# Attention products on 64-row groups, two PSUM banks per tile, units of four and five tokens, and routing in two halves

## The chip, the cores and the metric

The kernel runs on one core of one Trainium2 chip. The metric is the device time in microseconds of one execution. TensorE is called PE below, VectorE DVE, ScalarE ACT, GpSimd POOL and the DMA-issuing SyncE SP.

## The reference

Eight batches of eight heads with 576 positions of 64 elements, all in float32:

```python
def sm_attn(qq, kk, vv):
    s = scale * np.matmul(qq, kk.transpose(0, 1, 3, 2))
    s = s - np.max(s, axis=-1, keepdims=True)
    a = np.exp(s)
    a = a / (np.sum(a, axis=-1, keepdims=True) + 1e-09)
    return np.matmul(a, vv)
p_packed = sm_attn(p, k, v)              # 32 pooled keys for each head
out = sm_attn(q, p_packed, p_packed)     # 576 x 32 scores for each head
# x = out as (4608, 512); each token goes to its best expert of 8
expert_idx = np.argmax(xn @ en.T / tau, axis=1)
out[mask] = gate_w[mask, None] * (np.maximum(x[mask] @ w1[e], 0.0) @ w2[e])
# then a dense gated layer: (x @ w_a) * (x @ w_b) @ w_out
```

## The kernel before

The kernel has three stages. **Attention** (function `attention`) takes the batches one after another and leaves, for each, the normalized weights `a` of the second softmax (to `a_dram`) and the transposed pooled keys `ppT` (to `pT_dram`). The attention output itself is never formed: since out = a times p_packed, the first expert product is a times (p_packed times w1). **Experts** (class `Moe`, functions `zed`, `up_mm`, `down_mm`) runs 16 slots of 288 tokens, two per batch; `zed` makes z = p_packed times w1 once for each batch. It assumes that all tokens of a batch go to one expert, whose number SP reads into a register, and a slower path (`Dense`) is taken if that fails. **The gated layer** (class `Moe2`) follows; the change leaves it alone.

The order on each engine is fixed when the program is built: `Sched.run` places operations one after another, by planned durations, priorities (`prio`) and the number of free buffers (`take` and `free`). Each engine then works its list in order, and so does SP's queue of DMA issues.

In the attention stage `prep(b)` transposes pooled queries (`pT_mm`, L252) and keys (`kT_mm`, L272), forms the first scores (`s1_mm`, L302 and L307), takes their exponentials, transposes these (`eT_mm`, L356), multiplies by the values (`pp_mm`, L373), and makes `ppT` (L398) and the small Gram matrix `gr` (L412, L413, L417). `query(b)` transposes the queries (L458) and calls `rest(b, w)` for units of three tokens (a token here is one position index i of 9 on 64 partitions, for two halves of the partitions): second scores `s2_mm` (L496), maximum (L502), subtraction (L506), exponential (L510), sum and reciprocal (L514, L515), normalization (L519), transposition (L525), and the product `x_mm` (L539) with `gr`, from which squared norms (L548, L553) and router dots are taken. `experts(b)` (L672, L691 to L721) then routes one batch.

In the products for scores, for `x` and for `z`, one operand holds 64 useful rows per head. `s1_mm`, `s2_mm` and `zed` use all 128 rows of the array with zeros in the other half: `pz`, `pT` and `ppT` are padded with zeros so that a head of the lower or the upper half is picked by which half is zero. `x_mm` uses 128 rows with a block-diagonal `gr` of four blocks. Only `pp_mm` and `gr_mm` use 64-row groups. In the trace a 32-bit matmul other than a transposition makes two records, each with its own weight load.

PSUM has eight banks. In the attention stage four single banks are `tr` (transpositions, first scores, `gr`, routing, the first batch's z), two are `sm` (second scores, and the two halves of `pp`), two are `x`. In the experts stage three pairs of banks are `up`, two single banks are `dn`.

Of the kernel before, what the change touches and what calls it, by code (L numbers as in the profile page):

```python
# [22 lines left out]
NI = NT // 64  # L23
AHEAD = 0.65
QA = 1.5
# [9 lines left out]
def make_consts(nc, c, keep, pool, emb, tau, psum, en, esq):  # L35
# [7 lines left out]
    c.blk = pool.tile([128, 4, NP], F32, name="blk")  # L43
    nc.gpsimd.memset(c.blk, 0.0)
    for j in range(4):
        nc.gpsimd.memset(c.blk[32 * j:32 * j + 32, j, :], 1.0)
# [103 lines left out]
NW = CI // 3  # L150


def attention(ctx, tc, c, q, k, v, p, a_dram, pT_dram, consts, more):
    nc = tc.nc
    W = 4 * NP + E
    sizes = dict(tr=4, sm=2, x=2, k=3, v=3, q=3, qT=4, e=2, eT=2, a=2, an=3, aT=2, sq=2, pz=2, pT=2, kt=1,
                 pc=2, gr0=2, gr1=2, ppT0=2, ppT1=2, **{f"kT{m}": 1 for m in range(4)})
    sb = {}
    for name, pools in dict(io="kvq", kt=["pT", "kt"] + [f"kT{m}" for m in range(4)], q=["qT"], e=["e", "eT"],
                            pp=["pc", "gr0", "gr1", "ppT0", "ppT1"], x=["a", "an", "aT", "sq"]).items():  # L160
# [4 lines left out]
    ps_pool = dict(tr=c.ps_tr, sm=c.ps_sm, x=c.ps_x)  # L165
    pzs = [sb["pT"].tile([128, 2, 3 * D], F32, name=f"pz{i}") for i in range(2)]
    for t in pzs:
        nc.vector.memset(t, 0.0)
# [7 lines left out]
    own["a"] = [sb["a"].tile([128, 12, NP + 1], F32, name=f"as{i}") for i in range(sizes["a"])]  # L176
    for g in range(2):
        own[f"ppT{g}"] = [sb["pc"].tile([128, 4, 2, NP], F32, name=f"ppT{g}{i}") for i in range(sizes[f"ppT{g}"])]
        for t in own[f"ppT{g}"]:
            nc.gpsimd.memset(t, 0.0)  # L180
# [16 lines left out]
    def psum(n, key):  # L197
        T_[key] = ps_pool[n].tile([128, 512], F32, tag=n, name=n)
# [22 lines left out]
    def prep(b):  # L221
# [5 lines left out]
        def load_p(e):  # L227
            turn_ = T_["pz", b] = pzs[b % 2]
            nc.sync.dma_start(out=turn_[:, :, D:2 * D], in_=p[b].rearrange("(g j) p d -> (j p) g d", j=4))
# [17 lines left out]
        def pT_mm(e):  # L247
            ps = psum("tr", ("pTp", b))
            tile_("pT", ("pT", b), [128, 2, 2, 128])
            for g in range(2):  # L250
                for a in range(2):
                    nc.tensor.transpose(  # L252
                        ps[:, (2 * g + a) * 128:(2 * g + a + 1) * 128], T_["pz", b][:, g, (1 - a) * D:(3 - a) * D],
                        c.ident)

        def pT_ev(e):
            copy(e, T_["pT", b], T_["pTp", b].rearrange("p (g a q) -> p g a q", g=2, a=2))

        t, bpT = Buf("tr"), Buf("pT")
        o = op({"T": 0.44}, pT_mm, deps=[o_p], prio=at(0), take=[t, bpT], free=[bp])  # L260
        o_pT = op({"A": 0.47, "V": 0.6}, pT_ev, deps=[o], prio=at(0), free=[t])
# [28 lines left out]
        for g in range(2):  # L290
            def s1_mm(a, g=g):
                def f(e):
                    ps = psum("tr", ("s1p", b, g, a))
                    if (g, a) == (0, 0):
                        tile_("e", ("e", b), [128, CI, 2, D])

                    def w(j):
                        h = 2 * j + g
                        return T_["pT", b][:, h // 4, a, h % 4 * 32:h % 4 * 32 + 32]

                    for j in range(4):
# [3 lines left out]
                    if a == 0:  # L305
                        for j in range(4):
                            nc.tensor.matmul(  # L307
                                ps[32 * j:32 * j + 32, 256:320], lhsT=w(j),
                                rhs=T_["kT", b, 4][:, j, 64 * g:64 * g + 64], start=True, stop=True)
# [1556 lines left out]
```

## Time and profile before

| | us |
|---|---|
| median of 3 runs | 1373.44 (1370.06 to 1374.18) |
| the profiled execution | 1371.34 |
| its span, first to last instruction | 1369.5 |
| busy in the span: PE | 1335.0 |
| DVE | 790.8 |
| ACT | 591.9 |
| POOL | 106.5 |

The busy time of PE counts a matmul from its start to its modelled end, so that pipelined matmuls overlap in it; how long a matmul occupies PE is read from the start of one group to the start of the next. The clock column of the stretches is the granted share of full speed.

### The profile page before, as it was taken

To read this page: it belongs to the slowest core of one execution; us is meant where nothing else is said; L and a number is where in the kernel's file an instruction comes from. 1 tells how busy PE (TensorE), PEld (TensorE's weight loads), DVE (VectorE), ACT (ScalarE), POOL (GpSimd) and SP (SyncE) were. 2 spreads that over 40 slices of the span, in tenths; PEclk is the share of its full clock that TensorE was granted. 3 is DMA by queue.
4 is the path that set the end of the run, shared out by engine and by line. 5 is a ranking of instruction groups with operands and counts; after the bars stand their busy time and mean duration, and the time that the engine had idled before them with its cause. 6 is when DMAs were issued, how large, how long until landed. Compare 5 with 4: busy or idle time off the path is not lost. (4 is left out here: it accounts for less than half of the span.)

```text
span 1369.5 us, 26692 instructions
## 1 busy us (share of the span) xinstructions
PE 1335.0 (97%) x10263; PEld 1214.9 (89%) x10263; DVE 790.8 (58%) x1635; ACT 591.9 (43%) x1222; POOL 106.5 (8%) x234
## 2 busy tenths in 40 slices
PE   8998989999999999999999999999999999999997
PEld 6767778999999998999899999999999989999996
DVE  5787867666766655798554356434634363444342
ACT  5656524444444434565533244234433442343232
POOL 1121210101001000000100010001000010001001
PEclk9999999999999999999999999999999999999999
DMA  8878366778876735777865576557655665556552
GB/s 286 279 244 258 119 223 228 253 241 262 289 247 200 238 116 187 254 254 268 254 170 162 162 232 176 161 157 221 188 160 160 206 199 159 160 166 198 160 161 65
DMA packets 169272, 278.04 MB, mean 203 GB/s; under 512 B 16937, under 2 KB 68521, under 8 KB 169137
## 3 DMA queue, kind: packets, MB, share of 16 engines
q1 hardware_dynamic: 162704, 257.35, 60.9%
q0 software_dynamic: 6272, 18.88, 4.0%
q8 instruction: 84, 1.38, 0.4%
q14 instruction: 52, 0.42, 0.1%
q10 hardware_dynamic: 160, 0.02, 0.0%
HBM read 219.04 MB, written 57.15 MB: 202 GB/s over the span
## 5 line engine op out<-in xcount | busy, mean ns | idle before, releaser
L1443 DVE TENSOR_TENSOR s<-s,s 128x384 f32<-128x384 f32 x324 | 176.8, 556 | 340.8 <-ACT s L1579 338.4
L765 PE MATMUL pb<-xq,wq 128*128 128x384 f32 x504 | 170.2, 338 | 1.5 <-DVE s L1443 0.7
L765 PE MATMUL pa<-xq,wq 128*128 128x384 f32 x504 | 169.6, 337 | 1.6 <-DVE s L1443 1.6
L1692 PE MATMUL o<-oh,gh 128*128 128x512 f32 x432 | 170.3, 394 | 0.9 <-ACT osb L1712 0.9
L1693 PE MATMUL o<-ol,gh 128*128 128x512 f32 x432 | 170.4, 394 | 0.0
L1694 PE MATMUL o<-oh,gl 128*128 128x512 f32 x432 | 170.4, 394 | 0.0
L767 PE MATMUL pa<-xq,wq 128*128 128x384 f32 x504 | 170.3, 338 | 0.0
L767 PE MATMUL pb<-xq,wq 128*128 128x384 f32 x504 | 170.1, 337 | 0.0
L766 PE MATMUL pb<-xq,wq 128*128 128x384 f32 x504 | 170.0, 337 | 0.0
L766 PE MATMUL pa<-xq,wq 128*128 128x384 f32 x504 | 169.9, 337 | 0.0
L765 PE MATMUL dn<-hh,w2h 128*128 128x288 f32 x512 | 153.0, 299 | 0.0
L1579 ACT COPY s<-pa 128x384 f32<-128x384 f32 x180 | 86.5, 481 | 149.9 <-PE pa L767 149.8
L767 PE MATMUL dn<-hh,w2l 128*128 128x288 f32 x512 | 151.0, 295 | 0.0
L766 PE MATMUL dn<-hl,w2h 128*128 128x288 f32 x512 | 150.3, 294 | 0.0
L1579 ACT COPY s<-pb 128x384 f32<-128x384 f32 x180 | 86.5, 481 | 140.7 <-PE pb L767 140.6
L765 PEld LDWEIGHTS dn<-hh,w2h 128*128 128x128 f32 x512 | 96.1, 188 | 11.7 <-ACT w2h L994 5.9
L765 PEld LDWEIGHTS pb<-xq,wq 128*128 128x128 f32 x504 | 94.7, 188 | 11.8 <-DVE c L1443 1.6
L765 PEld LDWEIGHTS pa<-xq,wq 128*128 128x128 f32 x504 | 94.7, 188 | 10.0 <-DVE s L1443 2.2
L766 PEld LDWEIGHTS pb<-xq,wq 128*128 128x128 f32 x504 | 94.6, 188 | 8.4
L766 PEld LDWEIGHTS pa<-xq,wq 128*128 128x128 f32 x504 | 94.6, 188 | 7.5
L1694 PEld LDWEIGHTS o<-oh,gl 128*128 128x128 f32 x432 | 81.0, 187 | 18.8
L766 PEld LDWEIGHTS dn<-hl,w2h 128*128 128x128 f32 x512 | 96.8, 189 | 0.0
(192 smaller groups left out, 2436.1 us busy)
## 6 DMA issues: line engine op xcount, KB each, us to landing
wq<-ws SPq DMA_DIRECT2D x420, 256.0 KB, 2.8
ws<-wq SPq DMA_DIRECT2D x84, 256.0 KB, 3.7
raw<-in_moe_w_dram SPq DMA_DIRECT2D x36, 512.0 KB, 6.2
rawb<-in_moe_w_dram SPq DMA_DIRECT2D x28, 512.0 KB, 9.1
k<-in_k_dram SPq DMA_DIRECT2D x16, 576.0 KB, 5.4
v<-in_v_dram SPq DMA_DIRECT2D x16, 576.0 KB, 5.5
q<-in_q_dram SPq DMA_DIRECT2D x16, 576.0 KB, 5.1
xr<-x2T SPq DMA_DIRECT2D x20, 384.0 KB, 4.9
```

The lines of the kernel that those rows point to most:

```text
L765: nc.tensor.matmul(ps, lhsT=wh, rhs=xh, start=start, stop=False, **kw)
L766: nc.tensor.matmul(ps, lhsT=wh, rhs=xl, start=False, stop=False, **kw)
L767: nc.tensor.matmul(ps, lhsT=wl, rhs=xh, start=False, stop=stop, **kw)
L1443: VT = lambda out, a, b, o: V.tensor_tensor(out=out, in0=a, in1=b, op=o)
L1579: A.copy(out=T[n, key], in_=ps[n, names_bank[key]])
L1692: nc.tensor.matmul(a, lhsT=gh[:, h, s], rhs=wh, start=first, stop=False)
L1693: nc.tensor.matmul(a, lhsT=gh[:, h, s], rhs=wl, start=False, stop=False)
L1694: nc.tensor.matmul(a, lhsT=gl[:, h, s], rhs=wh, start=False, stop=last)
```

## The change

The first scores, the second scores, `x` and `z` are computed by 64-row matmuls, the lower heads on rows 0 to 63 and the upper heads on rows 64 to 127, issued in turn and written to two different banks. The zero padding goes: `pz` is loaded twice by DMA instead (two issues for each batch), `pT` and `ppT` shrink to half, `gr` has two blocks instead of four, and `keep` and `pr` move half the bytes in fewer issues. `sm` and `x` give way to `two`, two tiles of two banks each, which `s1`, `pp`, `s2`, `x` and the first batch's z share; `s1` leaves `tr`. The first scores are no longer copied to SBUF: the maximum and two exponentials (320 and 256 elements) read PSUM. A batch has two units, of four tokens (0, 2, 1, 3) and five (4, 6, 8, 5, 7), even and odd tokens in different banks. Routing runs twice, for batches 0 to 3 and 4 to 7: the first inside the attention stage, the second at the start of the experts stage. The fetch of the first expert's weights moves with it to a later place (priority 18.0 instead of 14.0, of 36).

```diff
-QA = 1.5
+QA = 2.0
...
-NW = CI // 3
+UNITS = ((0, 2, 1, 3), (4, 6, 8, 5, 7))
...
-            def s1_mm(a, g=g):
+            def s1_mm(e, g=g):
+                ps = psum("two", ("s1p", b, g))
...
+                def w(j, a):
+                    h = 2 * j + g
+                    return T_["pT", b][D * a:D * a + D, h // 4, h % 4 * 32:h % 4 * 32 + 32]
+                for j in range(4):
+                    for a in range(2):
                         nc.tensor.matmul(
-                            ps[32 * j:32 * j + 32, 0:256].rearrange("q (i p) -> q i p", i=4), lhsT=w(j),
-                            rhs=T_["kT", b, j][:, :, 64 * g:64 * g + 64], start=True, stop=True)
+                            ps[32 * j:32 * j + 32, a, 0:256].rearrange("q (i p) -> q i p", i=4), lhsT=w(j, a),
+                            rhs=T_["kT", b, j][D * a:D * a + D, :, 64 * g:64 * g + 64], start=True, stop=True)
...
-            o = op({"V": 0.94}, mx, deps=evs, prio=f(0.33))
-            o = op({"A": 0.97}, exp, deps=[o], prio=f(0.37))
+            o = op({"T": 0.7}, s1_mm, deps=[o_pT] + o_kT, prio=f(0.25), take=[t] if g else [t, be], free=[bpT] + bkT)
+            o = op({"V": 1.05}, mx, deps=[o], prio=f(0.33))
+            o = op({"A": 1.25}, exp, deps=[o], prio=f(0.37), free=[t])
...
         def s2_mm(e):
+            ps = psum("two", ("s2", t))
+            for i in range(0, banks[0][2], 4):
+                for j in range(4):
+                    for g in range(2):
+                        for a, _, m in banks:
+                            if i < m:
+                                x = tokens[banks[a][1] // 4 + i // 4] // 2
+                                nc.tensor.matmul(
+                                    ps[64 * g:64 * g + 64, a, (i + j) * NP:(i + j + 1) * NP],
+                                    lhsT=T_["qT", b, x][rows2[a], j, 64 * g:64 * g + 64],
+                                    rhs=T_["ppT", b, g][rows2[a], j, :], start=True, stop=True)
...
         def x_mm(e):
+            psum("two", ("xp", t))
+            for at, i in enumerate(tokens):
                 for g in range(2):
-                    off = 192 * w + 64 * i
-                    nc.tensor.matmul(ps[64 * g:64 * g + 64, i * W:i * W + W], lhsT=T_["aT", b][:, g, off:off + 64],
-                                     rhs=T_["gr", b, g], start=True, stop=True)
+                    for r in range(2):
+                        nc.tensor.matmul(xp()[64 * g:64 * g + 64, r, at],
+                                         lhsT=T_["aT", b][rows2[r], g, 64 * i:64 * i + 64],
+                                         rhs=T_["gr", b, g][rows2[r]], start=True, stop=True)
...
+            def mm(e, f=f, st=st):
+                st["ps"] = psum()
+                for j in range(4):
+                    for g in range(2):
+                        rows = slice(D * g, D * g + D)
+                        nc.tensor.matmul(st["ps"][32 * j:32 * j + 32, g, :], lhsT=self.pr[rows, j, :],
+                                         rhs=self.raw1[j][rows, f], start=True, stop=True)
...
-                for b in range(B - 1):
-                    e_ops, g_ops = experts(nc, c, tmp, b, tr)
-                    speak[b] = chain(S, e_ops, 4.5 * b + 4.5 + LG, x_ops[b], step=0.05)
-                moe.before(S, tr, 14.0, speak[0])
+                e_ops, g_ops = experts(nc, c, tmp, 0, KNOWN, tr)
+                e = chain(S, e_ops, 4.5 * KNOWN + LG, of(0, KNOWN), step=0.05)
+                speak.update({b: e for b in range(KNOWN)})
+                moe.before(S, lambda: c.ps_two.tile([128, 2, 512], F32, tag="two", name="two"), 18.0, e)
```

## Rows read from the trace of the kernel before

**Rows 1.** Stretches of the span: busy time of each engine, clock, DMA share, GB/s.
```profile
core 0: us, PE busy (x) PEld busy (x) DVE busy (x) ACT busy (x) POOL busy (x), PEclk, DMA share, GB/s
0.00:20.00 20.00, 13.43 (x234) 10.90 (x234) 8.85 (x28) 10.46 (x21) 3.73 (x21) 1.00 0.87 300
20.00:160.00 140.00, 132.55 (x2816) 102.62 (x2810) 109.96 (x340) 88.11 (x209) 27.86 (x26) 1.00 0.74 241
160.00:180.00 20.00, 15.08 (x356) 12.38 (x353) 18.18 (x64) 7.20 (x19) 2.63 (x2) 0.91 0.12 45
180.00:220.00 40.00, 37.42 (x262) 34.91 (x263) 21.51 (x51) 13.61 (x23) 3.47 (x3) 0.91 0.75 243
220.00:500.00 280.00, 279.91 (x2116) 259.05 (x2116) 191.58 (x298) 127.68 (x206) 24.62 (x34) 1.00 0.75 244
600.00:1360.00 760.00, 758.32 (x3927) 702.12 (x3926) 375.86 (x705) 295.42 (x628) 37.97 (x133) 1.00 0.61 182
```

**Rows 2.** PE's timeline in the attention stage: start, length, group, idle time before.
```profile
69.24 0.92 PE L539 MATMUL x<-gr,aT 128*64 128x136 f32 x12 [0.21 <-DVE aT L205]
70.09 0.33 PE L356 MATMUL tr<-ident,e 128*128 128x128 f32 x1
...
70.78 0.86 PE L373 MATMUL sm<-v,eT 64*32 64x64 f32 x64
71.57 0.55 PE L525 MATMUL tr<-ident,an 128*128 128x128 f32 x3
...
76.18 0.60 PE L252 MATMUL tr<-ident,pz 128*128 128x128 f32 x4
76.71 0.64 PE L302 MATMUL tr<-kT,pT 128*32 128x256 f32 x8
77.16 0.29 PE L307 MATMUL tr<-kt,pT 128*32 128x64 f32 x8
77.39 0.92 PE L539 MATMUL x<-gr,aT 128*64 128x136 f32 x12
...
78.49 1.13 PE L496 MATMUL sm<-ppT,qT 128*64 128x64 f32 x32
79.55 0.66 PE L458 MATMUL tr<-ident,q 128*128 128x128 f32 x4
...
80.50 0.64 PE L302 MATMUL tr<-kT,pT 128*32 128x256 f32 x8
81.07 0.66 PE L458 MATMUL tr<-ident,q 128*128 128x128 f32 x4
```

**Rows 3.** PE's timeline around one group of z products.
```profile
255.76 0.29 PE L767 MATMUL up<-ath,zl 128*128 128x288 f32 x1
255.99 1.92 PE L961 MATMUL up<-raw,pr 128*32 128x512 f32 x16
257.84 0.40 PE L765 MATMUL dn<-hh,w2h 128*128 128x288 f32 x1
258.08 0.30 PE L766 MATMUL dn<-hl,w2h 128*128 128x288 f32 x1
```

**Rows 4.** Instructions of line 961: nanoseconds, minimum, median, maximum.
```profile
L961 PE MATMUL up<-raw,pr x224: 592/592/617, 213.6 to 477.7; 128*32 128x512 f32 x112
```

**Rows 5.** Groups of instructions, 0 to 183 us: busy us, mean ns, idle before.
```profile
L502 DVE TENSOR_REDUCE mx<-sm 128x12 f32<-128x384 f32 x24 | 13.2, 549 | 5.7 <-PE sm L496 5.6
L321 DVE TENSOR_REDUCE mx<-e 128x1 f32<-128x576 f32 x16 | 11.7, 732 | 2.7 <-ACT e L203 2.7
L203 ACT COPY e<-tr 128x320 f32<-128x320 f32 x14 | 6.0, 426 | 5.1 <-PE tr L307 4.7
L417 DVE TENSOR_TENSOR gr<-tr,blk 128x128 f32<-128x128 f32 x16 | 4.3, 284 | 2.0 <-PE tr L413 2.0
L672 DVE TENSOR_TENSOR lg<-ndt,r 128x72 f32<-128x72 f32 x7 | 1.9, 266 | 0.0
```

**Rows 6.** DVE's timeline: ends of three holds of PSUM banks.
```profile
76.85 0.60 DVE L390 TENSOR_SCALAR pc<-sm,rs 128x128 f32<-128x128 f32 x2
...
78.45 0.55 DVE L548 TENSOR_TENSOR sq<-x,an 128x384 f32<-128x384 f32 x1
...
80.33 0.55 DVE L506 TENSOR_TENSOR as<-sm,mx 128x384 f32<-128x384 f32 x1
```

More of the change, by code (lines that the diff above doesn't have):

```diff
@@ L164, in attention @@
     st = ctx.enter_context(tc.tile_pool(name="a_st", bufs=4, side="right"))
[L165 to L168, printed above, removed]
+    ps_pool = dict(tr=c.ps_tr, two=c.ps_two)
     own = {n: [sb[n].tile([128, 2, CI + 1, D], F32, name=f"{n}{i}") for i in range(sizes[n])] for n in "kq"}
@@ L173, in attention @@
     en_mm, en_ev = consts(*(sb[n].tile([E, DM], F32, tag=n, name=n, bufs=sizes[n]) for n in ("e", "e")))
[L176 to L180, printed above, removed]
+    own["a"] = [sb["a"].tile([128, 20, NP + 1], F32, name=f"as{i}") for i in range(sizes["a"])]
     for t in own["a"]:
@@ L366, in f @@
                 if i0 == 0:
-                    for g in range(2):
-                        psum("sm", ("ppp", b, g))
+                    psum("two", ("ppp", b))
                 for i in range(i0, i1):
@@ L500, in mx, with scores @@
+        def scores():
+            v = lambda a, m: T_["s2", t][:, a, 0:m * NP].rearrange("p (x k) -> p x k", k=NP)
+            if even:
+                m = banks[0][2]
+                yield slice(0, 2 * m), T_["s2", t][:, :, 0:m * NP].rearrange("p a (x k) -> p a x k", k=NP)
+            else:
+                for a, at, m in banks:
+                    yield slice(at, at + m), v(a, m)
+        two = lambda v: v.rearrange("p (a x) k -> p a x k", a=2) if even else v
         def mx(e):
-            T_["mx2", t] = m = st.tile([128, 12], F32, tag="mx2", name="mx2")
@@ L509, in exp @@
+            T_["a", t] = T_["a1", t][:, :, 0:NP]
+            for s, x in scores():
+                nc.vector.tensor_tensor(out=two(T_["a", t][:, s]), in0=x, in1=two(wide(T_["mx2", t][:, s])),
+                                        op=ALU.subtract)
         def exp(e):
@@ L569, in rest @@
-        x = Buf("x")
-        o = op({"T": 0.86}, x_mm, deps=[o_T, gr_ops[b, 0], gr_ops[b, 1]], prio=f(0.7), take=[x],
+            nc.vector.tensor_reduce(out=c.n2[:, nd], in_=T_["sq", t], axis=AX.X, op=ALU.add)
+        B_ = {m: Buf(m) for m in ("a", "an", "sq", "two")}
+        f = lambda x: 4.5 * b + 2.0 * w + x
+        used = sorted({i // 2 for i in tokens})
+        V = lambda m, ops=1: 0.12 * ops + 0.0011 * m
+        m = 128 * n
+        o = op({"T": 0.215 * n}, s2_mm, deps=[o_qT[x] for x in used] + ppT_ops[b, 0] + ppT_ops[b, 1], prio=f(0),
+               take=[B_["two"]], free=[bqT[x] for x in used] + [T_["bppT", b, g] for g in range(2)])
@@ new lines, in rest @@
+        for i0, i1 in ((0, 4),) if w == 0 else ((4, 7), (7, 9)):
+            tr = Buf("tr")
+            o = op({"T": 0.125 * (i1 - i0)}, aT_mm(i0, i1), deps=[o_n], prio=f(0.5), take=[tr], free=[B_["an"]])
+            o_T.append(op(evict(128 * (i1 - i0)), aT_ev(i0, i1), deps=[o] + before[:1], prio=f(0.5),
+                          take=[] if w else [T_["baT", b]], free=[tr]))
+        x = Buf("two")
+        o = op({"T": 0.175 * n}, x_mm, deps=o_T + [gr_ops[b, 0], gr_ops[b, 1]], prio=f(0.7), take=[x],
@@ L977, in split_a @@
+            for g in range(2):
+                self.o_z[b, g, h] = o
     def split_a(self, S, s, p):
```

353 lines of the change are left out of this document (164 added, 189 removed).

## The prediction

> **What bounds the kernel now.** I read the page's busy times first, then the stretches, then PE's timeline. The chain that ended last holds only the final output stores and says nothing here. The stretches [rows 1] show three regimes. From 220 to 500 us (experts) and 600 to 1360 us (gated layer) PE is busy all the time, DVE and ACT two thirds or less, so each microsecond of PE work removed there comes off the end. From 20 to 160 us (attention) PE is busy for 132.6 of 140 us, DVE for 110.0, ACT for 88.1: PE sets the pace here too, with 7.4 us of idle time, but DVE follows closely. From 160 to 180 us it is the reverse: DVE 18.2 of 20 us, PE 15.1, the granted clock 0.91. This is the last batch's chain, and there PE work is not what counts. I take the attention stage as about 180 us, 22.5 us a batch. The gated layer is untouched, so the sum has an attention part and an experts part.
>
> **How long groups occupy PE.** In [rows 2], from start to next start: `x` for three tokens 69.24 to 70.09, 0.85 us; 64 records of `pp` 0.79; four `pT` transpositions 0.53; the first scores of one head group 0.45 + 0.23 for the first matmul set and 0.57 for the second, 1.25 together; second scores of three tokens 1.06. A z group: its neighbours are 0.13 apart, so it pushes the next ones from 255.89 to 257.95, 2.06 us [rows 3]. Its 16 records go through four column tiles, four rounds; the group lasts 1.92 us and one record 0.59 [rows 3, 4], so a round of 512 columns is (1.92 - 0.59)/3 = 0.44 us, 0.86 ns a column.
>
> **Do row groups overlap?** The change lives on that. `pp` already runs on 64 rows by 32 columns, eight tiles. A round of 64 columns is 0.055 us; on four tiles at a time 64 records would need 16 rounds, 0.88 us, and eight tiles 0.44 us, each plus a boundary of about 0.15 (what `x` takes beyond six rounds of 136 columns: 0.85 - 0.70). Measured: 0.79 [rows 2], under 1.03 and above 0.59. So they overlap, not perfectly where weight loads are as frequent as there. For long streams (z with 512 columns, `s1` with 256) I take full overlap.
>
> **Experts part.** z: eight tiles instead of four, two rounds instead of four, 2 x 0.44 = 0.89 us a group, two groups a batch. Seven batches lie in the saturated stretch [rows 1]: 7 x 1.77 = 12.4 us gained. Bound below: nothing, if row groups queued.
>
> **Attention part**, PE work:
> - `s1`: 16 records on eight tiles are two rounds, 0.57 as now for eight on four; with the 0.23 of the single tokens 0.80 instead of 1.25: 16 x 0.45 = 7.2 us.
> - `x`: now six rounds of 136 columns in pairs. Then eight records of 72 columns a token on four tiles, two rounds of 0.062: 0.65 and 0.77 us for the two units instead of 3 x 0.85: 1.13 x 8 = 9.0 us. If weight loads of two row groups queued, 2.53 us a batch: no gain.
> - `s2`: now 16 pairs in 0.91 us, 0.057 each. Since 32-column and 64-column matmuls alternate, I read this as the pace of weight loads. Then 16 records a token on four tiles: 1.06 and 1.29 us instead of 3 x 1.06: 0.83 x 8 = 6.6 us. If row groups queued, 4.40 instead of 3.18: a loss of 9.8 us. I take the overlap, as `pp` is nearer to it (0.79 us against 0.59 and 1.03 is in the middle, but with 32-column loads, two for each column).
> - `pT`: two transpositions fewer, 8 x 0.27 = 2.1 us. First batch's z: 1.8 us.
>
> Together 26.7 us (bound: 1.3).
>
> A rule that speaks against this: the Trainium skill, "TensorE: Matmul & The Clock Gate" (section on the 56 ns gap), says that matmuls never start closer than about 25 ns however short they are. The change makes matmuls shorter and more: `s2` from 768 to 1152 records, `x` from 288 to 576. By that floor, as an estimate from the page, the `s2` records alone would take 29 us, more than the 25 us they take now. The trace disagrees for different tiles: 64 records of `pp` in 0.79 us, 12 ns each [rows 2].
>
> **The other engines.** DVE: 24 units with five operations of 0.55 us become 16; slope from 128 elements at 0.284 to 384 at 0.549 [rows 5] is 1.03 ns an element, fixed 0.15, so 0.68 us at four tokens, 0.81 at five, and 0.15 more for the two that are cut by bank: 65.9 to about 62 us. Routing seven times has eight 72-element operations of up to 0.27 us, 15 us; once with 288 elements 0.49 each, 4 us. The maximum: 0.73 becomes 0.68 + 0.22, 2.7 us more. Net 12 us less. ACT loses 28 of the copies of scores at 0.43 or less and gets a second exponential of about that size: roughly even. So DVE goes from about 137 to 125 us in a stage of about 160, no fuller than today. DMA is busy for 0.74 of 20 to 160 us and 0.12 after [rows 1]; the same bytes in less time and batch 0's weights (4 MB) later use that slack.
>
> **Waits added.** Six users share two `two` tiles. Holds now: `s2` 78.49 to 80.88, 2.39 us; `x` 77.39 to 79.00, 1.61; `pp` 70.78 to 77.45, 6.67 [rows 2, 6]. Scaled by the sizes above, a batch then holds: `s2` 2.65 + 3.45, `x` 1.55 + 1.8, `pp` 6.7, `s1` twice 3.4 (product 0.8, maximum 1.1, two exponentials 0.85 from the 0.43 us copy of 320 elements [rows 5], handovers 0.6): 22.9 us, 11.5 for each tile, against 22.5 - 3.3 = 19.2 us of PE time a batch. That fits with 40% to spare, yet a hold that waits in DVE's queue delays PE, which works its list in order. Also SP's register load for batch 0 waits for the wider routing, with later q, k and v loads behind it. PE idles 7.4 us in 140 today; I give back as much again, 7 us (bounds: nothing, and all 26.7). At the end of attention the steps of routing leave DVE's list, but units are longer; I count nothing. The second routing (about 2 us more of DVE, a power on POOL of 36 columns) meets a DVE busy for 21.5 of 40 us [rows 1], and batch 4's weights are fetched a hundred microseconds later: nothing, or 5 us if PE's row products in the chain came before their input.
>
> **Sum.** 26.7 - 7 + 12.4 = 32.1 us. The profiled execution took 1371.3 (span 1369.5), 2.1 below the median: 1339.2 for it, 1341 as a median.
>
> **Rivals.**
> - The two tiles become the bound. From holds 1.67 times as long PE waits for them, at 1.96 times the attention stage is as long as now. Then only the experts part stays: 1361. For it: DVE at 79% in 20 to 160 us. Against: the slack worked out above. 0.11.
> - Slower: the same queue at more than 2.09 times (24.0 us a batch) eats the experts part as well; at 2.3 times attention takes 212 us, 32 more, and the time is 1393. It decides at 48 us of holds a batch. `pp` at 6.67 us, which waits in three steps for ACT's copies, shows how a hold can grow; nothing else does. 0.04.
> - Weight loads of two row groups queue: 1.3 + 12.4 us, 1360. 0.07.
> - Short matmuls are paced one by one, at twice the 12 ns of a `pp` record, whatever their tiles: `x` takes 2.1 us a batch and `s2` 3.9, the attention part gains 8.9, the time is 1352; `pp` itself contradicts it, 0.05. This is the floor of the Trainium skill's page named above.
> - The z matmuls do not overlap, so that part of the change does nothing: 24.9 - 7 = 17.9 us, 1356. `pp` speaks against it. 0.05.
> - The gains are lost in all, by these together: within 0.3% of now. 0.03.
>
> The forecast keeps 0.65, its own range 1328 to 1351 (give-back between nothing, and also a shorter end stage, and 17 us). With the rivals, 1328 to 1360 leaves out about 0.15. A measurement of this kernel tells about 0.3% from no change; faster 0.93, within 0.3% 0.03, slower 0.04.
>
> **What would show it.** A z group of about 1.2 us and the experts stage 12 us shorter with PE still full; `s1` 0.8 us a head group, `x` about 0.65 and `s2` 1.06 for four tokens; the first expert matmul some 20 us earlier; PE's idle time between 20 and 140 us near 14 us, ended by DVE or ACT at `two`. The prediction is wrong if `s2` for four tokens takes 1.7 us or more, if z stays at 2 us, if PE waits for `two` by more than 20 us, or if the granted clock falls in the attention stage, where it is 1.00 until 160 us.

## The result and the profile after

The changed kernel takes 1380.57 us (median of 15 runs) against 1372.87 us (15 runs of before on the same chip): 1.0053 times as long, 95% interval 1.0034 to 1.0073. It is slower by some 8 us where the prediction had it faster by 32. The profiled execution took 1377.84 us, its span is 1376.0 us, 6.5 more than before's.

The stretches of the changed kernel, to be read beside [rows 1]:

```profile
core 0: us, PE busy (x) PEld busy (x) DVE busy (x) ACT busy (x) POOL busy (x), PEclk, DMA share, GB/s
0.00:20.00 20.00, 12.88 (x220) 10.11 (x221) 7.86 (x29) 8.63 (x20) 2.43 (x17) 1.00 0.90 304
20.00:160.00 140.00, 116.95 (x3148) 95.87 (x3154) 90.08 (x242) 68.09 (x174) 19.05 (x12) 0.89 0.64 211
160.00:180.00 20.00, 15.23 (x459) 12.73 (x447) 13.46 (x24) 8.43 (x16) 1.05 (x1) 0.74 0.56 164
180.00:220.00 40.00, 34.84 (x455) 32.92 (x447) 27.63 (x56) 13.67 (x26) 8.93 (x4) 0.91 0.61 202
220.00:500.00 280.00, 277.49 (x2183) 264.34 (x2184) 196.38 (x302) 129.01 (x207) 24.86 (x35) 1.00 0.77 246
600.00:1360.00 760.00, 758.25 (x3926) 702.90 (x3925) 380.72 (x716) 295.06 (x630) 34.39 (x120) 1.00 0.62 183
```

From 20 to 160 us every engine is less busy than before: PE 117.0 us instead of 132.6, DVE 90.1 instead of 110.0, ACT 68.1 instead of 88.1, the DMA share 0.64 instead of 0.74. Nothing took PE's place as the bound. And PE's clock is 0.89 where it was 1.00, 0.74 instead of 0.91 in the next stretch.

Most of PE's groups of work have become as short as forecast. PE's timeline of the changed kernel, beside [rows 2] (the stretches are ones at full clock) and [rows 3]:

```profile
32.01 0.66 PE L294 MATMUL two<-kT,pT 64*32 64x256 f32 x16
32.46 0.31 PE L298 MATMUL two<-kt,pT 64*32 64x64 f32 x8
32.70 0.66 PE L264 MATMUL tr<-ident,k 128*128 128x128 f32 x4
...
89.14 1.14 PE L479 MATMUL two<-ppT,qT 64*64 64x32 f32 x64
90.21 0.66 PE L264 MATMUL tr<-ident,k 128*128 128x128 f32 x4
...
118.96 0.86 PE L547 MATMUL two<-gr,aT 64*64 64x72 f32 x40
119.75 0.44 PE L245 MATMUL tr<-ident,pz 128*128 128x128 f32 x2
120.55 0.73 PE L547 MATMUL two<-gr,aT 64*64 64x72 f32 x32 [0.36 <-ACT e L315]
121.22 1.20 PE L342 MATMUL tr<-ident,e 128*128 128x128 f32 x9
122.35 1.59 PE L479 MATMUL two<-ppT,qT 64*64 64x32 f32 x80
123.87 0.66 PE L720 MATMUL tr<-nd,pair 128*128 128x64 f32 x4
...
225.25 0.29 PE L797 MATMUL up<-ath,zl 128*128 128x288 f32 x1
225.47 1.95 PE L987 MATMUL up<-raw,pr 64*32 64x512 f32 x32
227.35 0.40 PE L795 MATMUL dn<-hh,w2h 128*128 128x288 f32 x1
```

From start to next start: first scores of a head group 0.69 us (before 1.25), second scores 1.07 for four tokens and 1.52 for five (1.06 for three), `x` 0.67 and 0.79 (0.85 for three), two z groups 2.10 less the usual 0.13, 0.98 each (2.06).

Between such groups PE stands still. The first large case, all five engines on one timeline:

```profile
18.52 0.63 PEld L358 LDWEIGHTS two<-v,eT 64*32 64x32 f32 x56 [0.17 <-issue]
18.52 0.78 PE L358 MATMUL two<-v,eT 64*32 64x64 f32 x55
18.62 0.58 ACT L196 COPY kT<-tr 128x512 f32<-128x512 f32 x1 [0.73 <-PE tr L264]
22.57 0.44 PE L358 MATMUL two<-v,eT 64*32 64x64 f32 x9 [3.28 <-issue]
22.57 0.20 PEld L358 LDWEIGHTS two<-v,eT 64*32 64x32 f32 x8 [3.43 <-issue]
22.94 0.71 PEld L264 LDWEIGHTS tr<-ident,k 128*128 128x128 f32 x4 [0.17 <-issue]
```

A group of 64 `pp` products stops after 55, and the last nine come 3.28 us later. They read the same `v` and `eT` and write the same tile as the 55, so no data and no bank was missing; "issue" is the profile's word for idle time in which PE waited for nothing that it shows. The other engines run dry meanwhile. The stretches around it show what follows (columns as above), and the DMA queues between 19.30 and 22.57 us what moved then:

```profile
19.30:22.57 3.27, 0.00 (x0) 0.00 (x0) 0.00 (x0) 0.00 (x0) 0.00 (x0) 0.99 0.44 152
22.57:29.30 6.73, 6.19 (x97) 4.80 (x97) 1.60 (x6) 2.02 (x4) 0.00 (x0) 0.50 0.45 114
29.30:36.00 6.70, 6.67 (x194) 5.76 (x193) 5.58 (x17) 4.79 (x14) 1.04 (x1) 1.00 0.84 271
```
```profile
DMA packets 234, 0.50 MB, mean 152 GB/s; under 512 B 25, under 2 KB 25, under 8 KB 233
## 3 DMA queue, kind: packets, MB, share of 16 engines
q1 hardware_dynamic: 233, 0.48, 42.3%
q8 instruction: 1, 0.02, 2.1%
```

Behind the stall the granted clock is at the lower of its two levels for 6.7 us, 0.50, then 1.00 again. And in the stall one packet of the queue "instruction" arrives, 16,384 bytes. Each of the ten "issue" stalls of over 0.3 us before the first expert matmul has such a packet beside it. From the DMA records of the changed kernel (us; the packet's start and end, PE's stall, and the time from the packet's end to PE's next matmul):

```
packet           stall            next matmul after
 20.14-21.26      19.29-22.57      1.31
 38.67-39.71      39.31-41.13      1.42
 48.49-49.54      49.04-51.00      1.46
 63.70-64.73      64.02-66.17      1.44
 78.80-79.77      78.36-81.29      1.52
101.69-102.78    101.21-104.12     1.34
112.75-113.82    114.19-115.11     1.29
134.55-135.49    135.75-136.85     1.36
143.31-144.25    145.22-145.67     1.42
150.34-151.37    150.36-152.78     1.41
```

The last column hardly varies. PE goes on 1.3 to 1.5 us after a packet has landed, whatever it was in the middle of: it had run out of instructions. The page's queue rows fit: 84 packets before, 89 after, and 688 matmuls with as many weight loads more (10,263 to 10,951), so a packet holds some 275 PE instructions (one packet more or less would make it 229 or 344; from the packet of 27.70 us to that of 189.87 us 30 packets brought 3725 matmuls with their weight loads, 248 each). What PE waited for until the first expert matmul, in the chain of waits (us in total, times, longest), five of the 18 lines:

```profile
PE two L358 <- issue: 9.6, 4, 3.3
PE tr L245 <- DMA pz<-in_p_dram: 5.0, 1, 5.0
PE two L479 <- DVE as L506: 3.9, 1, 3.9
PE two L294 <- issue: 3.1, 2, 2.2
PE two L547 <- issue: 2.9, 2, 1.8
```

All "issue" lines together are 20.2 us (before 2.7). Waits for DVE or ACT at a `two` tile are some 8 us, nearly half of them the one of 3.9 us in the last batch.

So the 6.5 us of the span split like this (stage by stage, after less before). The first expert matmul comes at 192.8 us instead of 182.8 (+10.0; forecast some 20 earlier). The experts take 332.4 instead of 340.1 us (-7.7; forecast -12.4). The gated layer, not touched, takes 850.8 instead of 846.6 (+4.2): at 541 us PE waits 3.55 us for `s` instead of 1.6, and the clock of 538 to 548 us is 0.84 instead of 1.00.

### The profile page after: what moved, and what is told of

Its sections match the earlier page's. It is cut to its first block, busy times and chain, and to the rows that moved or that the text cites. A ratio compares the mean times of both kernels' runs of the same rounds, so it can differ in the third digit from the quotient of the medians.

```text
span 1376.0 us, 27881 instructions
## 1 busy us (share of the span) xinstructions
PE 1319.0 (96%) x10951; PEld 1216.0 (88%) x10951; DVE 779.1 (57%) x1515; ACT 574.8 (42%) x1192; POOL 100.5 (7%) x216
## 3 DMA queue, kind: packets, MB, share of 16 engines
q8 instruction: 89, 1.46, 0.4%
## 4 chain that ended last, share of the span: by engine, by line
PE 87%; DMA 4%; DVE 4%; issue 2%; ACT 2%; POOL 0%; SPq 0%; ACTq 0%; DVEq 0%
PE o L1715 7%; PE o L1716 7%; PE o L1717 7%; PE pb L795 6%; PE pb L797 6%; PE pb L796 6%; PE pa L795 6%; PE pa L797 6%; PE pa L796 6%; PE dn L795 5%; PE dn L797 4%; PE dn L796 4%; PE up L795 2%; PE up L796 2%; PE up L797 2%
## 5 line engine op out<-in xcount | busy, mean ns | idle before, releaser
L1602 ACT COPY s<-pa 128x384 f32<-128x384 f32 x180 | 86.4, 480 | 151.8 <-PE pa L797 151.6
L797 PEld LDWEIGHTS dn<-hh,w2l 128*128 128x128 f32 x512 | 96.4, 188 | 0.0
```

The source lines that it names most:

```text
L797: nc.tensor.matmul(ps, lhsT=wl, rhs=xh, start=False, stop=stop, **kw)
L1602: A.copy(out=T[n, key], in_=ps[n, names_bank[key]])
```

## The experiments

**Theory (fetch):** PE consumes short products faster than packets of instructions arrive beside the loads of q, k and v; it stands still, and the clock falls behind the stalls (F in the expectations, S where it is about the clock). **Rivals:** products on 64 rows bring the clock down by themselves (C); late data, the shared `two` tiles or the ends of the stage hold PE (D).

One table for all runs, from the windows that begin with the span and end with the first expert matmul: idle is that time less PE's busy time, "issue" the part of it with that releaser, clock the mean granted clock, held back is half of the time in which PE was busy while its clock stood at 0.50 (44.0 us at that clock after, 40.0 of them busy; before 4.9 and 4.2), and the work is what is left, PE's work at full clock. The work is good to some 2 us: 6.8 us of products added in e12, e14 and e15 show in it as 5.5, 7.9 and 8.6.

| kernel | first expert matmul | idle | of it issue | clock | held back | work | median, ratio [95%] |
|---|---|---|---|---|---|---|---|
| before | 182.8 | 19.7 | 2.7 | 0.99 | 2.1 | 161.0 | 1372.87 |
| after | 192.8 | 38.8 | 20.2 | 0.89 | 20.0 | 134.1 | 1380.57, 1.0053 [1.0034, 1.0073] |
| e1_z | 183.9 | 20.1 | 3.0 | 0.98 | 3.9 | 159.9 | 1361.28, 0.9924 [0.9907, 0.9940] |
| e2_cut | 194.9 | 25.1 | 7.8 | 0.98 | 3.7 | 166.0 | 1380.2, 1.0062 [1.0047, 1.0077] |
| e3_pairs | 186.1 | 37.1 | 16.2 | 0.90 | 16.2 | 132.9 | 1368.56, 0.9982 [0.9971, 0.9992] |
| e4_thin_after | 178.4 | 29.1 | 8.9 | 0.91 | 13.5 | 135.8 | 1362.72, one run |
| e5_thin_before | 180.3 | 17.0 | 0.0 | 0.98 | 2.9 | 160.4 | 1368.96, one run |
| e6_z_s1 | 191.3 | 31.0 | 11.8 | 0.94 | 10.1 | 150.2 | 1369.15, 0.9978 [0.9966, 0.9991] |
| e7_z_route | 185.8 | 24.9 | 6.7 | 0.98 | 3.4 | 157.5 | 1369.41, 0.9978 [0.9964, 0.9992] |
| e8_pairs_x128 | 189.7 | 33.4 | 15.3 | 0.90 | 16.4 | 139.9 | 1369.34, 0.9977 [0.9965, 0.9988] |
| e9_thin_z_s1 | 178.0 | 23.5 | 3.8 | 0.98 | 2.9 | 151.6 | 1357.25, one run |
| e10_thin_cut | 184.1 | 18.1 | 1.9 | 0.98 | 2.7 | 163.3 | 1371.78, one run |
| e11_thin_pairs_x128 | 176.1 | 25.9 | 7.4 | 0.93 | 9.9 | 140.4 | 1357.13, one run |
| e12_after_shift64 | 192.7 | 32.8 | 16.2 | 0.88 | 20.3 | 139.6 | 1375.97, 1.0033 [1.0015, 1.0050] |
| e13_after_shift32 | 193.2 | 38.9 | 21.6 | 0.89 | 18.1 | 136.2 | 1381.14, 1.0075 [1.0049, 1.0102] |
| e14_z_shift64 | 192.7 | 22.0 | 4.2 | 0.98 | 2.9 | 167.8 | 1372.88, 1.0015 [0.9995, 1.0034] |
| e15_z_s1_shift64 | 189.5 | 26.8 | 7.0 | 0.98 | 3.9 | 158.8 | 1372.87, 1.0009 [0.9993, 1.0025] |

Read the second row against the first: the change took 26.9 us of work out of the stage (forecast 26.7), and put in 19.1 us of idle time and 17.9 us held back by the lower clock.

Two cautions. The stage's columns are those of one execution: that of e7_z_route and of e3_pairs is the fastest of 12, that of e8_pairs_x128 the slowest of 12, and the executions of the changed kernel lie between 1372.38 and 1385.64 us. And the medians come from several chips, on which the kernel before took 1370.96 to 1374.01 us, so two medians are compared to 2 or 3 us at best; the ratios are to the kernel before on the same chip.

**e1_z, z alone.** The kernel before with only the pooled keys' expert product on 64-row groups:

```diff
-                    for g in gs:
-                        for j in range(4):
-                            nc.tensor.matmul(st["ps"][32 * j:32 * j + 32, g - gs[0], :], lhsT=self.pr[0][g][:, j, g, :],
-                                             rhs=self.raw1[j][:, f], start=True, stop=True)
+                    for j in range(4):
+                        for g in gs:
+                            rows = slice(D * g, D * g + D)
+                            nc.tensor.matmul(st["ps"][32 * j:32 * j + 32, g - gs[0], :], lhsT=self.pr[rows, j, :],
+                                             rhs=self.raw1[j][rows, f], start=True, stop=True)
```

> The kernel before with the z products alone on 64-row groups (z, the unpadded copy of the pooled keys and its DMAs); attention as before. Theory F (fetch): the changed kernel lost its gain because PE runs out of instructions, which arrive in 16 KB packets of the instruction queue; z has as many matmul records as before, so F expects attention as long as before (first expert matmul at 182 to 185 us), z groups of 1.2 us, an experts stage some 12 us shorter and about 1361 us. Rival D (the ends of the stage absorb it, as the changed kernel's experts stage, only 7.8 us shorter, could mean): 1365 us or more.

1361.28 us. The experts' stage takes 328.3 us, 11.8 less than before. The long streams of z keep the whole of their forecast gain; z by itself lets attention be as long as before (first expert matmul at 183.9 us).

**e2_cut, more records, nothing else.** The kernel before with the products of `x` and the long first scores cut in two by columns, 544 records more on 128 rows:

```diff
-                    nc.tensor.matmul(ps[64 * g:64 * g + 64, i * W:i * W + W], lhsT=T_["aT", b][:, g, off:off + 64],
-                                     rhs=T_["gr", b, g], start=True, stop=True)
+                    for u in range(2):
+                        nc.tensor.matmul(ps[64 * g:64 * g + 64, i * W + 68 * u:i * W + 68 * u + 68],
+                                         lhsT=T_["aT", b][:, g, off:off + 64],
+                                         rhs=T_["gr", b, g][:, 68 * u:68 * u + 68], start=True, stop=True)
```

> The kernel before with x and the long first-score matmuls each cut in two by columns: same rows, same columns streamed, same output, 544 matmul records more in the attention stage (some 4 packets of instructions). F: PE's idle time put down to issue grows from 2.7 us to 8 or more within 205 us, the granted clock falls below 1.00 in places before 160 us, attention gets 8 to 20 us longer. Rival D (stalls come from late q, k, v data or from the shared PSUM tiles) and rival C (64-row matmuls lower the clock by themselves): nothing of that kind is in this kernel, at most 3 us longer.

The first expert matmul is 12.1 us later: 5.0 us more work, 5.4 us more idle (5.1 of it issue, which at 7.8 us ends just short of the 8 expected), 1.6 us at the lower clock. So more records of the same arithmetic bring stalls on 128 rows as well, with 88 packets instead of 84, while the clock stays at 0.98.

**e3_pairs, fewer records in the changed kernel.** Second scores by pairs of tokens on all 128 rows, with the zero-padded `ppT` of before; 512 records fewer:

```diff
-                                    lhsT=T_["qT", b, x][rows2[a], j, 64 * g:64 * g + 64],
-                                    rhs=T_["ppT", b, g][rows2[a], j, :], start=True, stop=True)
...
+                        nc.tensor.matmul(o, lhsT=T_["qT", b, tokens[i] // 2][:, j, 64 * g:64 * g + 64],
+                                         rhs=pT if k == 2 else pT[:, 0:1, :], start=True, stop=True)
```

> The changed kernel with second scores by pairs of tokens on 128 rows against zero-padded pooled keys, as before the change, units (0,1,2,3) and (4,5,6,7,8): 512 matmul records fewer, about 2 us more PE work, two half copies of the pooled keys more. F: issue idle falls from 19.9 us to 8 to 14, the clock recovers in part, attention 8 to 15 us shorter than the changed kernel's 192.8, about 1366 us. D and C: no shorter than the changed kernel, 1378 us or more.

12 us faster than the changed kernel by the medians, 10 by the ratios, issue idle 16.2 instead of 20.2 us. The time is near the 1366 us of F, but issue idle, clock (0.90) and attention (6.7 us shorter) miss what F had for them, and most of the loss stays. Its work is 1.2 us less than the changed kernel's, within the error: no saving of second scores on 64-row groups over pairs shows here.

**e4_thin_after and e5_thin_before, thin loads.** From the fourth on, each load of q, k and v brings only its first 64 columns, and the program's slower path is left out; the data are stale, the instructions are the same:

```diff
+    def part(n, dst, src):
+        seen[n] += 1
+        if seen[n] > 3:
+            dst, src = dst[:, :, 0:D], src[:, :, 0:D]
+        nc.sync.dma_start(out=dst, in_=src)
```

> The changed kernel; from the fourth load on, each half batch of q, k and v brings only 64 of 576 elements a partition (the rest of the tile is stale, so the output is not the reference's), and the slower path at the end is left out. Same instructions on PE. F with packets waiting behind data transfers: issue idle under 8 us, clock back, attention 165 to 175 us. F with the packet's own latency (1 us of transfer and 1.4 us until PE goes on): issue idle stays above 12 us. D (late data): issue idle under 3 us. C (clock by itself): the clock stays near 0.89 in 20 to 160 us whatever the idle time.

> The kernel before, with the key, query and value loads of the fourth and later batches cut down to a sliver, as in the thin version of the changed kernel (its outputs are then not the reference's, and the slower path of the program is left out). By the fetch theory the kernel before has hardly any fetch stalls to lose: its issue idle is 2.7 us before the first expert matmul, so that matmul moves from 182.8 us by less than 4 us for this reason; thin loads also start data-bound stages earlier, which should show as idle put down to DMA, not to issue. The thin version of the changed kernel had its first expert matmul at 178.4 us against 192.8 us: if the kernel before lands at 179 to 183 us with thin loads, the two kernels meet at about the same place once packets of instructions have the queues to themselves, and at least 10 of the 14 us that the thin loads gave the changed kernel were its own stalls. By the rival (thin loads help any kernel by shortening the data waits) the kernel before moves to about 169 us too, and the 14 us say nothing of the change.

The changed kernel wins 14.4 us in attention, 11.3 of its 20.2 us of issue idle among them; before wins 2.5. So some 12 us of the change's loss go with the loads. That the packets waited behind the data shows in the DMA records: with full loads three of the ten packets above started 0.4 to 0.9 us after PE had stopped, in e4 all nine had started 0.9 to 2.2 us before it did, and no stall is longer than 1.5 us. Still, all three numbers of F are missed (under 8 us, clock back, 165 to 175 us), and so are those of its second form and of D: 8.9 us of issue idle and a clock of 0.91 stay. The two kernels then end attention at nearly the same time (178.4 and 180.3 us), with 24.6 us less work in one of them: even without the loads, 12.1 us of idle time and 10.6 us of lower clock take most of it back.

**e6_z_s1.** z and the first scores (with pT) on 64-row groups, all else as before:

```diff
-                            ps[32 * j:32 * j + 32, 0:256].rearrange("q (i p) -> q i p", i=4), lhsT=w(j),
-                            rhs=T_["kT", b, j][:, :, 64 * g:64 * g + 64], start=True, stop=True)
...
+                            ps[a][32 * j:32 * j + 32, 0:256].rearrange("q (i p) -> q i p", i=4), lhsT=w(j, a),
+                            rhs=T_["kT", b, j][D * a:D * a + D, :, 64 * g:64 * g + 64], start=True, stop=True)
```

> The kernel before with two parts of the change alone: z on 64-row groups (as in the z-alone run, 1361.3 us) and the first scores and pT on 64-row groups in two banks, the token units, x, s2, the exponentials and the single routing per batch as before. The count of records of the first scores is the same as before, each is shorter, so TensorE is fed no more records but faster. By the fetch theory's weak form (stalls come when short records use up what was fetched) there are a few stalls of 2 to 3 us: issue idle 3 to 9 us, first expert matmul 177 to 182 us, time 1352 to 1361 us. By the clock theory (64-row products by themselves let the granted clock fall) the clock of 20 to 160 us falls below 0.96 although issue idle stays below 5 us, and the time is 1358 to 1370 us. By the sum of the prediction, without any stall, 1361.3 less 7.2 and 2.1, 1352 us.

Work falls by 9.7 us from e1_z to 150.2 (the sum had 9.3), and the kernel is 8 us slower: 10.9 us more idle, 8.8 of them issue, and 6.2 us more at the lower clock. That is worse than either theory had it. With nearly the same number of records (3395 and 3411), shorter ones are enough.

**e7_z_route.** z, and routing in two calls for four batches each, attention's products as before:

```diff
-                for b in range(B - 1):
-                    e_ops, g_ops = experts(nc, c, tmp, b, tr)
...
+                e_ops, g_ops = experts(nc, c, tmp, 0, KNOWN, tr)
```

> The kernel before with z on 64-row groups and with routing done twice (four batches, then the last four) in place of once per batch; no other product of attention changed. VectorE loses some 10 us of small work between 20 and 180 us, TensorE nothing. Theory: TensorE is the bound of this stage with 132.6 us busy of 140, so VectorE's relief is worth only the waits put down to it there (6.2 us before the first expert matmul at most), and the later start of the first weights and the second routing at the end take some back: 1357 to 1363 us against 1361.3 us of z alone. Rival (routing's tail at the end of attention is what costs the changed kernel its 10 us): the first expert matmul moves from 183.9 us to over 187 us and the time to over 1365 us.

Neither expectation fits: DVE is relieved (103.3 us busy from 20 to 160, 109.4 in e1_z), issue idle rises to 6.7 us, and the median of 1369.41 is 8 above e1_z, of which the profiled execution (1364.69, the fastest of 12) shows little. Relieving DVE is worth nothing here, so it was not what held PE. What costs the 8 us was not found.

**e8_pairs_x128.** e3_pairs with `x` on 128 rows too, 3257 records, fewer than before:

```diff
-                        nc.tensor.matmul(xp()[64 * g:64 * g + 64, r, at],
-                                         lhsT=T_["aT", b][rows2[r], g, 64 * i:64 * i + 64],
-                                         rhs=T_["gr", b, g][rows2[r]], start=True, stop=True)
+                        nc.tensor.matmul(xp(r, i0, i1)[64 * g:64 * g + 64, i - i0],
+                                         lhsT=T_["aT", b][:, g, 64 * tokens[i]:64 * tokens[i] + 64],
+                                         rhs=T_["gr", b, g], start=True, stop=True)
```

> The changed kernel with the second scores by pairs of tokens on 128 rows (as in the run before it, 1368.6 us) and with x back on 128 rows too, with four blocks instead of two; units of four and five tokens, exponentials from PSUM, routing twice and z on 64-row groups stay. Only pT and the first scores of attention are then on 64-row groups. About 290 records fewer than the pairs version, 800 fewer than the changed kernel, but x's records are about twice as long. By the fetch theory issue idle before the first expert matmul falls from 16.2 us to 6 to 12 us, the granted clock of 20 to 160 us rises from 0.90 to 0.94 or more, and x's extra 5 to 9 us of TensorE work are paid from that: 1358 to 1368 us. By the clock theory (any 64-row product pulls the clock down) the clock stays at 0.90 or below while issue idle falls, and the time is 1366 to 1376 us. By the sum of the prediction, where x costs its 9 us and stalls are nothing, it would be slower than the pairs version by 9 us, 1377 us.

The time lies where the clock theory had it, but issue idle did not fall at all (15.3 us, 11.8 of it in the `pp` groups), which neither expected. The count of records by itself does not set the stalls. In the traces they fit better with how close the short records stand: in this kernel all 144 `pp` products of a batch come in a row twice, and in the 4 us ahead of its three longest stalls PE started 196, 135 and 146 products against a mean of 74 in 4 us of the stage (changed kernel: 135, 184 and 175 against 92). No run varies that alone.

**e9, e10, e11: thin loads in e6_z_s1, e2_cut and e8_pairs_x128** (the edit of e4, with the same work left out):

> The kernel with z and the first scores on 64-row groups, with the key, query and value loads of the fourth and later batches cut to a sliver (outputs then not the reference's, the slower path left out). With full loads it idled 11.8 us at issue before the first expert matmul and ran 23.7 us at half clock; the kernel before with thin loads idles 0 us at issue and runs 6.3 us at half clock. Theory S (the clock falls because of the stalls): with thin loads issue idle falls below 5 us and half-clock time below 11 us, first expert matmul 173 to 177 us. Theory C (64-row products by themselves bring the clock down): issue idle falls below 5 us and half-clock time stays above 15 us, first expert matmul 178 to 184 us.

> The kernel before with the long products of x and the first scores cut in two by columns (544 records more, all on 128 rows, no other change), with the same thin loads. With full loads its first expert matmul was at 194.9 us against 182.8 us of before, 7.8 us of issue idle. If packets of instructions that wait behind data are the cause, issue idle falls below 3 us and the first expert matmul to 180 to 187 us, the rest being TensorE time of the added records. If the fetch is too slow by itself for so many records, issue idle stays above 5 us and that matmul comes after 188 us. Half-clock time stays near 8 us by either.

> The changed kernel with the second scores by pairs of tokens on 128 rows and x on 128 rows, with the same thin loads. With full loads it idled 15.3 us at issue and ran 37.5 us at half clock. Its attention has pT and the first scores alone on 64-row groups. Theory S: issue idle below 6 us, half-clock time below 15 us, first expert matmul 172 to 178 us. Theory C: issue idle below 6 us, half-clock time above 20 us, first expert matmul 178 to 184 us.

In e9 the issue idle falls from 11.8 to 3.8 us and the clock comes back to 0.98, with z and the first scores on 64 rows: 64-row products by themselves do not lower it. In e10 issue idle falls from 7.8 to 1.9 us and the first expert matmul comes 10.8 us earlier. Both as the fetch theory said, except that e9's matmul is at 178.0 and not before 177. In e11 issue idle falls from 15.3 to 7.4 us only, and the clock stays at 0.93: between the two. It has about the idle time of e2_cut (25.9 and 25.1 us) and nearly three times the loss of clock (9.9 and 3.7 us). Its trace says why. 4.4 of the 7.4 us are one stall, where loads run that the edit leaves full: four of 512 KB for the first expert, issued from 119.2 to 121.7 us. PE stops at 125.03 us, the packet that it lacks starts at 127.11 and ends at 128.02. The stretch before the stop, and the stall up to and from the packet's start (columns as above):

```profile
119.00:125.03 6.03, 5.82 (x235) 5.38 (x235) 5.93 (x16) 3.22 (x10) 0.51 (x1) 1.00 0.75 256
125.03:127.11 2.08, 0.00 (x0) 0.00 (x0) 0.06 (x1) 0.00 (x0) 0.54 (x1) 1.00 0.86 327
127.11:129.39 2.28, 0.00 (x0) 0.00 (x0) 0.00 (x0) 0.00 (x0) 0.00 (x0) 0.70 0.05 9
```

And of the 9.9 us held back, 5.6 stand behind waits for POOL and DVE near the end of the stage (2.96 and 3.23 us) and not behind stalls for packets.

**e12 to e15: where the packets' boundaries fall.** By the phase theory the place of the boundaries decides how long PE stands still in all, by the texture theory the order of work alone. One transposition at the very start repeated 64 times (32 in e13), so that all later boundaries shift by about half (a quarter) of a packet:

```diff
-        for i in range(4):
+        for i in [0] * 64 + list(range(4)):
             nc.tensor.transpose(c.en_ps[:, i * E:(i + 1) * E], en[:, i * 128:(i + 1) * 128], c.ident[:E, :E])
```

> The changed kernel with one 8x8 transposition at its start repeated 64 more times (64 products with their weight loads, same result): 128 TensorE instructions more, about half of the some 275 that one packet holds (1376 instructions more brought 5 packets more). Its own cost is at most 1.6 us. Phase theory: the issue idle of 20.2 us before the first expert matmul falls to 5 to 15 us or rises over 25 us, and the time goes with it, at least 5 us either way. Texture theory: issue idle 17 to 23 us at other places of the order, time within 3 us of the changed kernel's (ratio 1.003 to 1.008).

> The changed kernel with the same transposition repeated 32 more times, about a quarter of a packet; its own cost is at most 0.8 us. Phase theory: issue idle and time differ from those of the changed kernel and of the half-packet shift by several microseconds. Texture theory: issue idle 17 to 23 us, time within 3 us of the changed kernel's.

> The kernel before with z alone on 64-row groups, and the 64 added transpositions at the start. It had 3.0 us of issue idle and 1361.3 us. Phase theory: its boundaries lay well by chance, so half a packet's shift brings issue idle to 6 us or more and the time to 1366 us or more. Texture theory: issue idle below 5 us, time 1361 to 1364 us, the added products' own cost included.

> The kernel with z and the first scores on 64-row groups, and the 64 added transpositions at the start. It had 11.8 us of issue idle and 1369.2 us. Phase theory: half a packet's shift moves issue idle by 4 us or more, down to 3 to 8 us if its boundaries lay badly, and the time to 1360 to 1366 us. Texture theory: issue idle 9 to 14 us, time 1368 to 1372 us.

The added products cost more than I had allowed. PE's timeline at the start of e14_z_shift64:

```profile
4.55 1.09 PE L252 MATMUL tr<-ident,pz 128*128 128x128 f32 x4 [4.55 <-POOL en L54]
6.33 7.42 PE L63 MATMUL enps<-ident,e 8*128 8x8 f32 x68 [0.68 <-DVE e L57]
13.67 2.61 PE L272 MATMUL tr<-ident,k 128*128 128x128 f32 x11
```

68 of them take 7.34 us to the next start where four took 0.52 (e1_z), 6.8 us of own cost (107 ns each), not 1.6; in e13, where 36 take 3.93 us, 3.4. Less that, the medians are 1369.2 (e12), 1377.7 (e13), 1366.1 (e14) and 1366.1 (e15), against 1380.6, 1380.6, 1361.3 and 1369.2 without the shift: 11 and 3 us better, 5 worse, 3 better (by the ratios 10, 1, 5 and 3). The stalls stand at other places in all four (e14: 2.27 us at 63.8 and none at 121 us, where e1_z had its 2.87 us). Their sum moves by 1 to 5 us: 16.2 and 21.6 us against 20.2 in the changed kernel, 4.2 against 3.0, 7.0 against 11.8. The issue idle of e13 and e14 lies where the texture theory had it, that of e15 where the phase theory had it, that of e12 between the two. So the changed kernel keeps 16 to 22 us and the order of before with z alone 3 to 4 wherever the boundaries fall: that difference is in the orders themselves. That phase decides the place and some microseconds is argued only, as one execution of each was traced, and executions of one kernel differ by 10 us and more in time. The added time also shifts PE against the loads, which these runs do not separate.

## Why the prediction was wrong

**Right: the work.** The stage's PE work fell by 26.9 us where the sum had 26.7. First scores gained 16 x (1.25 - 0.69) = 9.0 us (7.2), `x` 8 x (2.55 - 1.46) = 8.7 (9.0), second scores 8 x (3.18 - 2.59) = 4.7 (6.6; the unit of five tokens takes 1.52 us, not 1.29). That the total is so near is in part luck, as the work is good to some 2 us only. The overlap of two row groups, on which the change lives, is there. z measured 0.98 us a group (0.89 in the sum, 1.2 among the signs) and 11.8 us in e1_z (12.4).

**Right: the other engines.** Four and five tokens cost DVE what was worked out (this is the list of groups by line, each shape apart, 0 to 193 us):

```profile
L558 DVE TENSOR_TENSOR sq<-two,an 128x640 f32<-128x640 f32 x7 | 5.7, 817 | 2.3 <-ACT nd L196 2.3
L558 DVE TENSOR_TENSOR sq<-two,an 128x512 f32<-128x512 f32 x8 | 5.5, 684 | 2.0 <-ACT nd L196 2.0
```

0.68 and 0.82 us, forecast 0.68 and 0.81. DVE as a whole went from 137.5 to 121.8 us before the first expert matmul (forecast 137 to 125); ACT, put down as even, lost 16 us. The rival in which the `two` tiles become the bound did not come: some 8 us of waits at them, where it asked for over 20. The rival of weight loads in a queue fell with `x` and z, and the one of products paced one by one with the second scores: 64 records in 1.07 us, 16.7 ns each. The Trainium skill, "TensorE: Matmul & The Clock Gate" (section on the 56 ns gap), has no start-to-start below about 25 ns; this trace, with products on different tiles, does not agree.

**Wrong: the step "I give back as much again, 7 us".** It allowed for waits on DVE and ACT and no others, and took the clock at 1.00 as before. The idle time grew by 19.1 us, of which 17.5 was issue: PE out of instructions. The rows of before had a trace of it, 2.7 us of issue in the list of waits, and I read neither that nor the "instruction" queue. And the lower clock, which the prediction named only among the things that would make it wrong and put at nothing in the sum, held back 17.9 us more than before. With these two in the sum attention is -26.9 + 19.1 + 17.9 = +10.1 us, measured 10.0. The end of the stage, for which the prediction counted nothing, has a part in it: of the 20.0 us held back, 12.7 stand behind the five issue stalls of over 2 us, 1.6 behind a short wait for ACT and a short issue stall, and 5.7 behind waits for DVE in the last batch (3.9 and 2.1 us; before, all 2.1 us held back stand behind such waits, of 1.6 and 3.0).

**How far the cause is shown.** That PE ran dry of instructions: shown by the group that stops after 55 of its 64 products, by the packet beside each of the ten stalls, by stalls that come with added or shorter records (e2_cut, e6_z_s1) and shrink with thin loads (e4, e9, e10, e11). That the lower clock follows the stalls: shown for e6_z_s1 against e9, where the loads were taken away, and most of the stalls with them. In the changed kernel it rests on the order in time. All kernels with its order of work (units of four and five tokens, shared tiles) lie at 0.88 to 0.93, also e11 with 25.9 us of idle time, while those with the order of before lie at 0.98 or 0.99 with up to 26.8 us (e15), but for e6 at 0.94. Issue stalls are one part of that. The longer waits of that order for DVE and POOL in the last batches are another, with 5.6 to 7.0 us held back behind them in the changed kernel, e4, e8 and e11 against 2.1 before: in all 17 traces each of the 71 stretches at the lower clock before the first expert matmul begins during idle time of PE or right behind it, whatever ended that. Not each idle time has one behind it: those of 1.82 and 1.96 us in the changed kernel have none. Why the stalls of that order are so many with fewer records (e8) stays open.

**Wrong in a small way: experts and the layer behind.** 4.1 of z's 11.8 us are missing. The second routing, put at nothing, runs 24 small products on PE in the middle of a stage that PE bounds, from 197.80 to 200.39 us, 2.6 us where the routing of one batch took 0.2 before; and PE waits 3.9 us for `hl` where it waits 2.1 in e1_z. The half clock at the start of the stage (to 196.6 us) is not the reason: 3.8 us of this stage's PE time ran at it, in e1_z 5.2. The gated layer's 4.2 us lie partly in the wait for `s` and the clock behind it. No run separates these.

**The better kernel** is e1_z, z alone: 0.9924 [0.9907, 0.9940] of before.

## What to carry to other kernels

Work taken from a busy PE by making products shorter is not yet time: look up the "instruction" queue and the "issue" idle time, and ask how fast the new order eats a packet of some 250 to 275 instructions while loads fill the DMA engines. Gains from long streams (z, 512 columns) arrive, gains from many short ones may not. And when a stage lives on a full clock, each added idle time is to be priced at its length and once more as work at half clock behind it: here 19.1 us of idle time brought 17.9 us of the second.

## What the runs showed of the hardware

PE goes on 1.29 to 1.52 us after a 16,384-byte packet of instructions has landed, in ten of ten cases, and the packet itself takes 0.94 to 1.12 us, so a stall that begins when the packet starts lasts some 2.4 us. In the changed kernel the granted clock went to 0.50 behind each of its five issue stalls of over 2 us, for 3.4 to 6.8 us. With thin loads, 19 of the 20 packets beside a stall (e4, e9, e10, e11) had started at least 0.86 us before PE stopped; the other one started 2.08 us after, with 327 GB/s of data on the DMA engines. 64 transpositions of 8 columns, one after the other into the same place, took 107 ns each (e12, e14), while products on different tiles followed each other at 12 to 17 ns (`pp` before, second scores after).
